# Linear attention and a routed expert layer on one core: one transfer per output tile, two x blocks per slot, a load moved to another queue, and a new written order

## The chip, the cores and the metric

The kernel runs on one core of a Trainium2 chip. The core has a matrix engine (TensorE, PE in the profile; its weight loads stand apart as PEld), a vector engine (DVE), a scalar engine (ACT), a general engine (GpSimd, POOL) and a queue engine (SyncE, SP). Each works through its own list of instructions in order and waits on semaphores for the others. Data moves between the device's memory and the on-chip memory by 16 DMA engines; transfers are issued from SP and ACT (hardware queues) and from POOL (a software queue, which can also convert the type on the way). The metric is the device time of one execution in microseconds (us).

## The reference

For 8 batches and 8 heads, with 576 positions and 64 columns a head, linear attention is computed with phi(x) = x + 1 for x > 0 and exp(x) otherwise; its result, 4608 rows of 512, is the input x of a layer of 8 experts, each of which works on every row:

```python
kv = einsum('bhsd,bhse->bhde', phi(k), v);  z = sum_s phi(k)
x  = (phi(q) @ kv) / (phi(q) . z + 1e-06)          # 4608 x 512
P  = exp(x @ w_gate - max), then 8 rounds of: rows / row sums, columns / column sums * N / E
out = sum over e of  P[:, e] * (relu(x @ w1[e]) @ w2[e])     # w1: 512x1024, w2: 1024x512
```

All inputs are float32; the kernel computes in float16 with float32 sums.

## The kernel before

**Planner.** The kernel does not issue its instructions in program order. Every piece of work is a task, added with `add` (engine, function, dependencies, priority, and the buffers it takes, `acq`, or uses, `use`); `_Plan.run` then emits the tasks engine by engine. A load is two tasks: the issue on `sp` or `pool`, and its time on a pretended engine `dma`. The order of the first part, to about 318 us, is written out in `_FRONT` (lines 139 to 213): each word is a task's number and a letter for the engine (p TensorE, a ACT, d DVE, g GpSimd, s SyncE, m dma, n none). What comes after it is chosen greedily, from the durations that each `add` states, by earliest start and then by priority. These durations and the dma tasks only shape the order. On the chip an engine waits for real semaphores: for data, and for a buffer's earlier readers.

**Attention** (`att`, 16 calls, one for each batch and group of four heads; below, the n-th k, q and v are those of call n, from 0). k, q and v come in as loads of 128 partitions. k goes into three float32 buffers `kin`, and so does q of call 0; the other q and all v are converted to float16 on the way by the software queue. Call 0's k and q and call 1's k are issued from SP (`sp = wide and b == 0`, line 370), all other loads from POOL, as are the weights. Then come exp on ACT (`ek`, `eq`), phi on DVE (`t`, `tq`), kv sums (`kv_ps`), the transposition of q (`att`, `qpT`), denominators (`rden`) and the x columns (`xT`). Before the first data PE runs 46 warm-up products.

**Experts.** Rows are taken in 9 units of 512. Expert 0 runs among the attention as far as its x is there: units 0 to 3 as plain products, later units in a form that does 7 block products in place of 8 on sums and differences of blocks, made by DVE. For experts 1 to 7 all units use the 7-product form. Its 7 blocks of x (the raw ones and the sums) are stored once per unit to a buffer in device memory (`xd`, by `x_blocks`) and loaded again for each expert by `x_load`, from SP, into a ring of ten slots `xs`. Units are grouped `SUBS = (0), (1,2), (3,4), (5,6), (7,8)`; a pair's block is one load of 256 KB, unit 0's is 128 KB and fills half of a slot. An expert thus takes 35 slots. `l1_half` takes a group's 7 loads and does the first layer (L801; `pair` holds the 7 products, read in the order 1, 5, 6, 3, 2, 7, 4); `layer2` does the second (L1095), with DVE adding P times the result into `acc` (L1126) and, for one of the seven products, ACT scaling and POOL adding (L1133, L1136). Slots 7 to 9 lie where `xT` and the routing's buffers were and open (`x_closed`) only when the routing weights `P_sb` are done, at the end of eight rounds on DVE that run beside expert 0.

**Weights.** w1 and w2 have two buffers each. A load is issued by POOL when the buffer of two experts before is free, and stands in POOL's order among the additions of L1136. Expert 0's come in halves (`parts=2`).

**End.** After the last expert's layer 2 each of a unit's four tiles of 128 rows by 512 is written out by `out_dma`: two transfers of 64 partitions, both from SP, and for unit 8 the second from ACT. Unit 8's last work (`last`) is done as five pieces, the last two of 256 columns each.

Of the kernel before, what the change touches and what calls it, by code (L numbers as in the profile page):

```python
# [17 lines left out]
class _Plan:  # L18
# [35 lines left out]
    def run(self):  # L54
# [85 lines left out]
1n 2p 3p 4p 0g 80g 5p 52g 6p 48s 49m 7p 8p 9p 10p 11p 12p 13p 14p 15p 16p 17p 76s 50s  # L140
51m 18p 19p 54a 20p 21p 22p 61n 23p 108n 78g 24p 25p 26p 27p 28p 29p 30p 31p 55d 62a 56d 63d 64d
65p 77m 82a 83d 84d 66a 53m 57n 58p 59a 60a 32p 33p 34p 35p 36p 79m 89n 90a 91d 67p 68a 81m 595n
85n 86p 92d 120g 118g 119m 37p 122g 148g 146g 109g 38p 87a 88d 121m 125d 69p 70a 71a 123m 39p 93p 94d 111g
40p 41p 74p 75d 42p 149m 124a 126d 150g 174g 176g 95p 96a 43p 44p 72p 45p 110m 73d 147m 127n 131n 133d 132a
159n 46p 97p 47p 98a 99a 113n 134d 202g 178g 128p 112m 114g 151m 206g 175m 160a 129d 161d 130d 135p 136d 177m 187n
596p 597p 100p 116g 101d 137p 138a 162d 179m 115m 207m 203m 598p 599p 139p 140a 102p 153d 103d 152a 154d 155n 141a 204g
205m 232g 106g 234g 233m 235m 163p 164a 600p 602p 604p 601d 603d 104g 605d 117m 156p 157a 606p 608p 158d 181d 144p 145d
180a 182d 236g 609a 165p 188a 166a 105m 237m 610p 607a 142p 143d 260g 261m 612p 167p 189d 190d 168a 169a 613d 183n 184p
185d 186d 191p 192d 611a 618p 172p 173d 262g 614p 615d 193p 194a 208a 170p 171d 107m 245n 263m 209d 210d 215n 217d 211n
632n 216a 616p 195p 633p 196a 634d 635p 636a 197a 246a 238a 218d 212p 213d 214d 637p 638d 219p 220d 200p 639p 292g 290g  # L150
247d 248d 201d 239d 240d 221p 222a 291m 641p 640a 642a 264g 617p 223p 293m 224a 225a 265m 198p 199d 624d 267d 241n 619p
249p 250d 273n 266a 242p 243a 244d 626a 620p 643p 320g 294g 318g 346g 274a 268d 275d 276d 348g 322g 321m 251p 252a 303n
226p 621p 644a 297d 227d 253p 622p 645p 319m 349m 296a 254a 228p 304a 646a 229d 298d 305d 269n 230p 270p 231a 271d 255a
277p 350g 376g 295m 278d 272a 374g 323m 375m 377m 331n 332a 333d 406g 647p 648a 258p 259d 666p 279p 280a 628a 256p 306d
257d 623p 281p 282a 283a 299n 665n 300p 630d 307p 301d 308d 378g 302d 324a 667a 347m 379m 359n 351m 360a 325d 361d 334d
668p 651p 309p 310a 284p 285d 326d 362d 669a 670p 653p 311p 312a 286p 287d 327n 654p 380a 335p 336d 328p 661a 313a 329d
330a 288p 289a 381d 560d 404g 407m 405m 493g 671d 353d 652p 352a 408g 460g 494m 314p 315d 337p 659a 338a 561d 672p 674p
675d 673a 339p 316p 354d 317d 355n 387n 389d 388a 491g 382d 390d 676p 678p 409m 461m 469s 462g 340a 677a 492m 463m 341a
470s 356p 363p 364d 464g 465m 471s 500s 417n 357a 679a 358a 501s 680p 410a 342p 343d 365p 366a 649p 562d 419d 344p 345d
553d 367p 368a 418a 681a 699p 383n 384p 385a 411d 386d 554d 369a 495g 496m 502s 563s 432g 433m 434g 435m 655p 391p 392a  # L160
372p 373d 412d 701p 656p 370p 371d 420d 497a 393p 394a 445n 413n 650p 414p 698n 700a 436g 415d 498d 499d 416d 702a 657a
395p 503g 396a 564m 555d 556s 558s 397a 663a 438a 437m 703p 682p 421p 400p 705p 684p 422d 439d 423p 704a 424a 401d 446a
447d 440d 574d 575d 557m 685p 398p 399d 683p 576d 577s 578m 559m 441n 476n 477a 425p 706d 426a 707p 708a 448d 692d 442p
443a 444a 709p 449p 478d 690d 450d 427a 508n 509a 479d 567d 688p 689p 451p 710a 428p 429d 581d 568d 582d 452a 569d 570s
572s 565s 571m 566m 686p 711p 453p 696a 454a 455a 466a 430p 431d 583d 713p 584s 579s 585m 588g 589n 480p 481d 510d 504n
592n 573m 687p 456p 457d 511d 712d 402p 505p 739n 403a 506a 593g 714d 507a 694d 467d 468d 512p 740p 590g 458p 459d 472n
741a 580m 513a 742p 744p 591m 514p 515a 473p 735d 474d 475d 736d 516p 517a 518a 719p 720p 482p 483a 743a 519p 520d 727d
721p 484p 485a 521p 745d 522d 737d 746p 722p 486a 747a 489p 715p 490d 738d 487p 488d 551n 731d 778d 1009s 1011s 748p 749a
729a 750p 752p 751a 779d 732d 780d 523p 524a 754p 552p 716p 733d 526d 753a 755a 786p 717p 723a 787a 525n 527p 586s 1013s
1015s 781s 800p 718p 790p 756d 734d 792p 785n 1017s 725a 791a 1010m 587m 788p 793a 801a 789a 760p 761a 836d 757d 837d 758d  # L170
528d 838d 783s 1019s 1021s 839s 796p 529d 759d 784m 804p 805a 806p 807a 766p 767a 782m 794p 802p 803a 810p 795d 797d 811d
762p 763a 840m 1022m 1014m 808p 809d 1001d 770p 771d 768p 530p 1002d 769d 531d 798p 812p 799a 813a 772p 773a 844p 845a 764p
894d 814d 846p 847a 848p 850p 858p 852p 843n 849a 859a 765a 851a 532d 815d 816d 820p 860p 818p 861a 866p 895d 853d 817d
819a 864p 854p 865a 533p 896d 897s 855d 867d 534d 824p 825a 868p 869d 862p 863a 535d 856p 857a 821a 828p 829d 870p 871a
902p 903a 826p 822p 952d 872d 827d 953d 1003d 823a 954d 955s 1012m 1018m 956m 873d 1004d 906p 830p 831a 908p 916p 876p 841s
899s 957s 909a 912p 536p 874d 537d 918p 901n 907a 875d 917a 922p 920p 594m 878p 898m 877a 919a 921a 904p 905a 923a 882p
883a 880p 881a 879a 926p 924p 538d 886p 913d 914p 927d 925d 887d 915a 910p 539p 540d 911d 884p 960p 961a 888p 889a 928p
962p 963a 959n 966p 964p 541d 885d 929a 930d 967a 965a 968p 969d 542p 543d 974p 975a 934p 970p 978p 976p 931d 971d 1020m
1016m 958m 980p 935a 977a 979a 981a 940p 972p 973a 936p 984p 544d 545p 982p 941a 932d 546d 983d 1023p 1024a 938p 985d 1025p
547d 1029p 986p 944p 937a 939a 1026a 945d 1030a 1031p 1027p 842m 900m 987a 548p 1033p 946p 947a 1028a 933d 942p 549d 1034d 1035p  # L180
1037p 1038a 988p 550d 1000n 625a 1036a 1032d 1513n 943d 1005d 1006d 1051s 1053s 1055s 1057s 1052m 1039p 989p 1043p 1054m 1514g 1056m 990p
1040a 629a 1044a 691d 1045p 1041p 996d 1047p 1065p 1048d 1042a 693d 1059s 1066a 631a 1061s 1060m 1058m 1062m 1063s 1147s 1149s 1064m 1067p
991p 1068a 1046d 1049p 992p 1071p 1072a 1073p 1069p 1074d 1075p 1050a 951a 1076d 774d 997d 1121d 1070a 993p 1077p 1079p 1081p 1078a 695d
1080a 1082a 994p 1085p 1087p 1083p 1086a 627a 1007d 1122d 728a 1084a 1089p 1088d 1123d 1090d 998d 1093p 1094a 1095p 1148m 1096a 1515m 995p
999a 1091p 1092a 1099p 1101p 1097p 1008d 1100a 1124d 1102d 1125p 1126a 1127p 1129d 1128d 1130p 1103p 1104d 1133a 1134g 1098a 1135p 1138p 1151s
1152m 1516n 1150m 1136d 1137d 1105p 1106a 1107p 1109p 1108a 1110a 1153s 1155s 1154m 1141p 1142d 1143d 1113p 1115p 1114a 1139d 1111p 1117p 1161p
1163p 1144p 834d 1116d 1118d 1119p 1157s 1131a 1112a 1156m 1162a 1167p 660a 1159s 1140d 662d 1146d 1145d 1269s 1271s 1164a 1169p 1165p 1120a
1189d 1168a 1193p 1195p 891a 1158m 1190d 1191d 1194a 664a 1198p 1201a 1166a 892a 658a 1171p 697d 1203p 1160m 1202g 1197d 1196d 1192d 1206p
1172d 1173p 1132g 1199a 1519d 1200g 1175p 1177p 1204d 1205d 1174a 1176a 1209p 1181p 1178a 1183p 1179p 1207d 1517g 1170d 1211d 1208d 1210d 1182a
# [27 lines left out]
def kernel(  # L217
# [553 lines left out]

    xst_of, xse_done, sx_users = {}, [], []

    n_load = [0]

    def x_load(d, blk, prio):
        gr = S_.grp(p_xs)
# [533 lines left out]
```

## Time and profile before

| | |
|---|---|
| median of 3 runs | 959.66 us (959.45 to 959.77) |
| the profiled execution | 959.16 us |
| its span, first to last instruction | 957.4 us |
| granted TensorE clock, mean | 0.999 |
| DMA traffic | 112.65 MB in 87908 packets |
| x loads `xs<-xd`, from SP | 196 of 256 KB, 49 of 128 KB |
| `out_dram<-acc` | 69 from SP, 5 from ACT |
| k loads `kin<-in_k_dram` | 2 from SP, 14 from POOL |

The page gives each engine's busy time and its share of the span, the span in 40 slices of about 24 us (a digit is the busy share in tenths), the DMA queues, the chain of work that ended last (followed back from the last instruction to what released it at each step), and groups of instructions with their count, mean duration and the idle time ahead of them. Times within the trace count from the span's start. A row of the timeline has its start, its length, engine, line, operation, what it writes and reads, and in brackets the idle time before it and what ended that. A matmul's modelled length includes its way through the array, so 0.44 us of issue shows as a row of 0.59.

### The profile page before, as it was taken

How to read it: one execution, taken by the hardware profiler on the slowest of the kernel's cores; microseconds unless marked ns; L12 is line 12 of the kernel's file. 1: busy time of each engine (PE TensorE's matmuls, PEld its weight loads, DVE VectorE, ACT ScalarE, POOL GpSimd, SP SyncE). 2: the span in 40 equal slices, each digit the busy share in tenths (PEclk: the TensorE clock that was granted, in tenths of full speed). 3: DMA queues.
4: the chain of work that ended last, by engine and by line, in shares of the span. 5: the costliest groups of instructions: out<-in, count | busy, mean ns of one | idle time of the engine just before them, and what ended most of it. 6: DMA issues, size and time to landing. Idle time of an engine off the chain costs nothing.

```text
span 957.4 us, 18335 instructions
## 1 busy us (share of the span) xinstructions
PE 945.6 (99%) x7008; PEld 651.5 (68%) x7008; DVE 774.1 (81%) x1499; ACT 581.8 (61%) x1034; POOL 146.3 (15%) x208
## 2 busy tenths in 40 slices
PE   8999999999999999999999999999999999999997
PEld 4565588666677666766677666766667666776665
DVE  6998999778987888778888888878887888877775
ACT  6899766676655555555555555555555555555552
POOL 6432000001111111111111111111112111111110
PEclk9999999999999999999999999999999999999999
DMA  9998663525136222652217321552217422125544
GB/s 246 262 238 208 157 163 95 154 78 122 61 75 147 77 79 61 176 121 77 63 48 163 89 78 61 139 115 71 76 49 170 116 79 61 56 78 165 165 134 132
DMA packets 87908, 112.65 MB, mean 118 GB/s; under 512 B 7436, under 2 KB 51468, under 8 KB 87820
## 3 DMA queue, kind: packets, MB, share of 16 engines
q1 hardware_dynamic: 63708, 76.77, 26.0%
q0 software_dynamic: 23712, 34.19, 19.2%
q8 instruction: 55, 0.90, 0.4%
q10 hardware_dynamic: 400, 0.52, 0.2%
q14 instruction: 33, 0.27, 0.1%
HBM read 119.69 MB, written 17.69 MB: 143 GB/s over the span
## 4 chain that ended last, share of the span: by engine, by line
PE 90%; DMA 4%; ACT 3%; DVE 2%; issue 1%; SPq 0%; POOL 0%; DVEq 0%
PE ye L1095 36%; PE hq L801 24%; PE R L801 12%; PE Zye L801 6%; PE Zye L1095 6%; PE ye L979 2%; PE hq L696 1%; DMA hb<-in_q_dram 1%; DMA w<-in_moe_w_dram 1%; DMA kin<-in_q_dram 1%; ACT eq L456 1%; DMA xs<-xd 1%; ACT rden L492 1%; PE kv_ps L422 1%; DVE xT L507 0%
## 5 line engine op out<-in xcount | busy, mean ns | idle before, releaser
L1126 DVE SCALAR_TENSOR_TENSOR acc<-ye,P_sb,acc 128x256 f32<-128x256 f32 x620 | 267.2, 479 | 126.6 <-PE ye L1095 124.5
L1095 PEld LDWEIGHTS <-S 128*128 128x128 f16 x1984 | 194.0, 98 | 46.6 <-DVE S L1066 0.2
L1095 PE MATMUL ye<-T,S 128*128 128x256 f16 x1488 | 192.8, 273 | 0.0
L1136 POOL TENSOR_TENSOR acc<-acc,st 128x256 f32<-128x256 f32 x124 | 88.9, 737 | 632.7 <-ACT st L1133 632.7
L1095 PEld LDWEIGHTS <-hb 128*128 128x128 f16 x1584 | 155.0, 98 | 42.7 <-issue 0.8
L801 PEld LDWEIGHTS <-W 128*128 128x128 f16 x1248 | 122.1, 98 | 86.8
L832 ACT ACTIVATE hb<-hq 128x512 f16<-128x512 f32 x134 | 80.0, 597 | 138.6 <-PE hq L801 133.8
L801 PE MATMUL hq<-xs,W 128*128 128x512 f16 (+1 forms) x560 | 150.0, 358 | 0.0
L801 PE MATMUL R<-xs,W 128*128 128x512 f16 (+1 forms) x560 | 150.0, 358 | 0.0
L801 PE MATMUL hq<-xs,w 128*128 128x512 f16 (+1 forms) x560 | 139.8, 358 | 1.3 <-DMA xs<-xd 1.3
L801 PEld LDWEIGHTS <-w 128*128 128x128 f16 x936 | 91.5, 98 | 60.9 <-issue 1.8
L829 ACT ACTIVATE hb<-Zye 128x512 f16<-128x512 f32 x134 | 80.1, 598 | 37.9 <-PE Zye L801 37.8
L835 DVE CUSTOM_DVE_ANT_0 hb<-hq,sx 128x512 f16<-128x512 f32 x126 | 86.6, 687 | 16.8 <-PE hq L801 16.8
L1133 ACT ACTIVATE st<-Zye,P_sb 128x256 f32<-128x256 f32 x124 | 52.5, 471 | 75.6 <-PE Zye L1095 75.6
L822 ACT COPY sx<-hq 128x512 f32<-128x512 f32 x126 | 73.6, 584 | 37.1 <-PE hq L801 37.1
L835 DVE CUSTOM_DVE_ANT_0 hb<-R,sx 128x512 f16<-128x512 f32 x126 | 86.4, 685 | 8.9 <-ACT sx L822 8.9
L818 ACT COPY Zye<-hq 128x512 f32<-128x512 f32 x134 | 77.8, 581 | 21.0 <-PE hq L801 20.8
L1066 DVE TENSOR_TENSOR S<-hb 128x1024 f16<-128x1024 f16 x124 | 84.9, 685 | 4.8 <-ACT hb L832 4.7
L801 PE MATMUL Zye<-xs,w 128*128 128x512 f16 (+1 forms) x280 | 75.0, 358 | 0.0
L826 ACT COPY sx<-R 128x512 f32<-128x512 f32 x126 | 74.4, 591 | 0.0
L1095 PE MATMUL ye<-w,hb 128*128 128x256 f16 x528 | 68.4, 273 | 0.5 <-DVE acc L1126 0.5
L1095 PE MATMUL Zye<-w,hb 128*128 128x256 f16 x528 | 68.4, 273 | 0.0
(119 smaller groups left out, 981.4 us busy)
## 6 DMA issues: line engine op xcount, KB each, us to landing
xs<-xd SPq DMA_DIRECT2D x196, 256.0 KB, 3.8
out_dram<-acc SPq DMA_DIRECT2D x67, 128.0 KB, 2.4
w<-in_moe_w_dram POOLq DMA_DIRECT2D x16, 512.0 KB, 7.9
kin<-in_k_dram POOLq DMA_DIRECT2D x14, 576.0 KB, 8.2
w<-in_moe_w_dram POOLq DMA_DIRECT2D x7, 1024.0 KB, 9.6
xs<-xd SPq DMA_DIRECT2D x49, 128.0 KB, 2.6
vv<-in_v_dram POOLq DMA_DIRECT2D x16, 288.0 KB, 7.2
hb<-in_q_dram POOLq DMA_DIRECT2D x15, 288.0 KB, 7.8
```

Source lines behind the costliest of these rows:

```text
L801: nc.tensor.matmul(dst_[:, p, :] if parts == 2 else dst_.rearrange("p a b -> p (a b)"), lhsT=lhs(p, c), rhs=blk[i](c), start=(first and p ...
L818: nc.scalar.copy(out=Zt[1], in_=gX["tile"])
L822: nc.scalar.copy(out=gs2["tile"], in_=gX["tile"])
L826: nc.scalar.copy(out=gs5["tile"], in_=gR["tile"])
L829: nc.scalar.activation(out=dst(0, 0), in_=Zt[1], func=AF.Relu)
L832: nc.scalar.activation(out=dst(1, 0), in_=gX["tile"], func=AF.Relu)
L835: nc.vector._custom_dve(TENSOR_ADD_SAT, out=out_, in0=ps, in1=sb, s0=3.0e38, s1=0.0)
L1066: nc.vector.tensor_tensor(out=Sx[:, i], in0=a0, in1=a1, op=op)
L1095: nc.tensor.matmul(bank(g_)[:, s, :], lhsT=lhs(s, kk), rhs=rhs(kk), start=(new and s == 0 and kk == 0), stop=(kk == 3), skip_group_check=True)
L1126: nc.vector.scalar_tensor_tensor(out=dst(), in0=bank(g_)[:, s, :], scalar=P_sb[:, gg, e:e + 1], in1=dst(), op0=ALU.mult, op1=ALU.add)
L1133: nc.scalar.mul(out=gst["tile"], in_=bank(g_)[:, s, :], mul=P_sb[:, gg, e:e + 1])
L1136: nc.gpsimd.tensor_tensor(out=dst(), in0=dst(), in1=gst["tile"], op=ALU.add)
```

## The change

1. **Output.** `out_dma` makes one transfer of 128 partitions per tile, or per piece of the last unit, in place of two of 64. Of `last`'s five pieces the second and fourth are issued from ACT, the others from SP.
2. **x blocks.** For unit 0 two blocks share a slot (each contiguous in its half), so its seven loads take four slots; an expert takes 32. The slots are numbered as before, round the ring of ten.
3. **Second k.** Call 1's k is issued from POOL; call 0's q and k stay on SP.
4. **Expert 2's weights** depend, in the plan, on the x loads of the first pair of expert 1.
5. **Plan.** Among dma tasks that could start, the one that became ready first is taken, not the one of lowest priority number. Some stated durations differ (x load issue 0.45 for 0.37, weight load 1.3 for 1.4, earliest start of the first software loads 4.2 for 5.2, half a dma time for a 128 KB x load).
6. **`_FRONT`** is written anew. On SP, call 0's q comes ahead of its k. POOL's order begins k1, identity, v0, q1, k2, v1, q2, q3, v2, expert 0's w1 first half, k3, w1 second half, v3, k4, q4, v4, w2 first half, k5, gate half, q5, v5, q6, k6, w2 second half; it was identity, v1, v0, q1, q2, k2, v2, q3, k3, w1 first half, w1 second half, v3, k4, q4, k5, v4, w2 first half, v5, w2 second half. Expert 2's w1 load stands on POOL behind four additions of expert 1 (units 0 and 1) in place of ahead of them; its w2 load, which stood behind those four, behind one addition more. On TensorE the first expert products keep their place after the first three calls' sums; from the 67th task to the 76th, and from about the 350th on, the two orders agree.

```diff
@@ _Plan.run
-                    if r is not None and at(e, t, r) <= te + 1e-9 and (pick is None or (t["prio"], t["id"]) < (pick["prio"], pick["id"])):
+                    if r is not None and at(e, t, r) <= te + 1e-9 and (
+                            pick is None or (t["ready"] if e == "dma" else t["prio"], t["id"]) <
+                            (pick["ready"] if e == "dma" else pick["prio"], pick["id"])):
@@ _FRONT
-1n 2p 3p 4p 0g 80g 5p 52g 6p 48s 49m 7p 8p 9p 10p 11p 12p 13p 14p 15p 16p 17p 76s 50s
...
+50s 51m 1n 61n 63d 2p 3p 4p 5p 6p 7p 8p 9p 48s 49m 10p 11p 76g 77m 62a 64d 55d 12p 13p
...
@@ att
-            sp = wide and b == 0
+            sp = n == 0 and wide
@@ x_load
-    def x_load(d, blk, prio):
-        gr = S_.grp(p_xs)
-        i = n_load[0] % NXS
-        n_load[0] += 1
-
-        def fn(_):
-            gr["tile"] = xs_t[i]
-            nc.sync.dma_start(out=xs_t[i][:, :, 0:len(SUBS[d])], in_=xd[d][:, blk])
...
+    def x_load(d, prio):
+        gx = {}
+        dbl = len(SUBS[d]) == 2
+        for m, (blk, b) in enumerate(ORD.items()):
+            h_ = 0 if dbl else m % 2
+            if h_ == 0:
+                gr = S_.grp(p_xs)
+                i = n_load[0] % NXS
+                n_load[0] += 1
+
+            def fn(_, gr=gr, h_=h_, i=i, b=b):
+                gr["tile"] = xs_t[i]
+                nc.sync.dma_start(out=xs_t[i] if dbl else xs_t[i][:, h_], in_=xd[d][:, b] if dbl else xd[d][:, b, :, 0])
...
+            def view(c, gr=gr, h_=h_):
+                return gr["tile"][:, c].rearrange("p s t -> p (s t)") if dbl else gr["tile"][:, h_, c]
+            gx[blk] = gr, td, view
+        return gx
@@ l1_half
-            st["x"] = {i: x_load(d, b, un) for i, b in ORD.items()}
+            st["x"] = x_load(d, un)
+            if n == 1:
+                first_x.extend(t for _, t, _ in st["x"].values())
@@ out_dma
-    def out_dma(g, tt, deps, c0=0, cw=DM):
-        for half in range(2):
-            def f_o(_, half=half):
-                bb, j = divmod(2 * (4 * g + tt) + half, NJ)
-                dst = AP(tensor=out.tensor, offset=(S * bb + j) * DM + c0, ap=[[NJ * DM, PW], [1, cw]])
-                eng = nc.scalar if g == NG - 1 and half == 1 else nc.sync
-                eng.dma_start(out=dst, in_=acc[g][64 * half:64 * half + 64, tt, c0:c0 + cw])
-            add(("sp", 0.45), f_o, deps=deps, prio=900.0)
+    def out_dma(g, tt, deps, c0=0, cw=DM, act=False):
+        def f_o(_):
+            o0, o1 = (S * bb + j for bb, j in (divmod(2 * (4 * g + tt) + half, NJ) for half in range(2)))
+            dst = AP(tensor=out.tensor, offset=o0 * DM + c0, ap=[[(o1 - o0) * DM, 2], [NJ * DM, PW], [1, cw]])
+            (nc.scalar if act else nc.sync).dma_start(out=dst, in_=acc[g][:, tt, c0:c0 + cw])
+        add(("sp", 0.5), f_o, deps=deps, prio=900.0)
@@ last
-            out_dma(g, tt, [t], c0, cw)
+            out_dma(g, tt, [t], c0, cw, act=i % 2 == 1)
@@ weights of later experts
-                w_t[e] = load_w1(e, prio=float(e), deps=w_t[e - 1][1][1:]) + load_w2(e, prio=float(e), deps=w_t[e - 1][3][1:])
+                w_t[e] = load_w1(e, prio=float(e), deps=w_t[e - 1][1][1:] + (first_x if e == 2 else [])) + load_w2(e, prio=float(e), deps=w_t[e - 1][3][1:])
```

More of the change, by code (lines that the diff above doesn't have):

```diff
@@ L145 @@
[L145 to L164, printed above, removed]
@@ new lines @@
+14p 15p 54a 56d 16p 17p 18p 0g 19p 20p 21p 65p 22p 595n 23p 24p 25p 26p 27p 83d 28p 82a 52g 53m
+57n 58p 59a 29p 30p 60a 66d 31p 32p 33p 84d 78g 79m 89n 90a 91d 92d 118g 119m 125d 67p 68a 34p 35p
+36p 37p 38p 39p 80g 81m 85n 124a 126d 120g 121m 113n 131n 69p 70a 40p 41p 86p 87d 71a 88d 42p 93p 132a
+43p 94d 148g 149m 122g 123m 74p 75d 108n 159n 109g 110m 95p 96a 44p 45p 146g 147m 72p 133d 73d 97p 98a 134d
+127n 128p 129d 161d 111g 112m 99a 130a 160a 135p 136d 46p 47p 150g 151m 174g 175m 100p 101d 596p 137p 138a 597p 598p
@@ new lines @@
+139p 176g 177m 178g 179m 102p 140a 599p 162d 153d 103d 114g 115m 152a 154d 155n 187n 202g 203m 163p 164d 600p 602p 604p
+605d 106g 107m 204g 205m 141a 601a 603a 156p 157d 158d 206g 207m 606p 608p 180a 181d 144p 145d 165p 182d 609a 166a 188a
+610p 611a 142p 143d 189d 190d 183n 215n 167p 612p 168a 169a 613d 184p 185d 186a 191p 192d 607a 614p 615a 172p 173d 193p
+194a 616p 170p 171d 209d 208a 210d 211n 234g 235m 232g 233m 116g 117m 262g 263m 236g 237m 632n 195p 618p 196a 633p 635p
+634d 260g 261m 217d 212p 216a 197a 218d 636a 213a 214d 637p 638d 219p 220a 200p 201d 639p 641p 642d 640a 245n 239d 221p
@@ L210 @@
[L210 to L212 removed]
+1626a 1629p 1658d 1631p 1659d 1630a 1627p 1691d 1633p 1628a 1632d 1663p 1665p 1634d 1664a 1660p 1692d 1666a 2089d 1635p 2086n 2087g 2088m 1669p
@@ L317, in load_w @@
             w_part[nm] = ti
-            ts_.append(add(("dma", len(part) * (1.4 if len(part) * len(pieces) > 2 else 2.6)), lambda _: None, deps=[ti],
+            ts_.append(add(("dma", len(part) * (1.3 if len(part) * len(pieces) > 2 else 2.6)), lambda _: None, deps=[ti],
                            use=[g, *gsw], prio=prio, lat=2.15))
@@ L387, in att @@
             tin[nm] = fadd(("dma", 1.47 if wide else 1.42), lambda _: None, deps=[ti], use=[gr, *gsw], prio=pr, lat=2.2,
-                           after=0.0 if sp else 5.2)
+                           after=0.0 if sp else 4.2)
         ge, gt = S_.grp(p_ek), S_.grp(p_t)
@@ L772 @@
     xst_of, xse_done, sx_users = {}, [], []
-    n_load = [0]
-    def x_load(d, blk, prio):
-        gr = S_.grp(p_xs)
-        i = n_load[0] % NXS
-        n_load[0] += 1
-        def fn(_):
-            gr["tile"] = xs_t[i]
-            nc.sync.dma_start(out=xs_t[i][:, :, 0:len(SUBS[d])], in_=xd[d][:, blk])
-        ti = add(("sp", 0.37), fn, acq=[gr], deps=[t for g in SUBS[d] for t in xd_done[g]] +
-                 [t_close, xs_prev[0], x_closed[0] if i >= 7 else None], prio=prio)
-        xs_prev[0] = ti
-        return gr, add(("dma", 1.0), lambda _: None, deps=[ti], use=[gr], prio=prio, lat=2.6)
+    n_load, first_x = [0], []
+    def x_load(d, prio):
[10 more added lines that the diff above has]
+                nc.sync.dma_start(out=xs_t[i] if dbl else xs_t[i][:, h_], in_=xd[d][:, b] if dbl else xd[d][:, b, :, 0])
+            ti = add(("sp", 0.45), fn, acq=[gr] if h_ == 0 else [], use=[gr] if h_ else [], deps=[t for g in SUBS[d] for t in xd_done[g]] +
+                     [t_close, xs_prev[0], x_closed[0] if i >= 7 else None], prio=prio)
+            xs_prev[0] = ti
+            td = add(("dma", 1.0 if dbl else 0.5), lambda _: None, deps=[ti], use=[gr], prio=prio, lat=2.6)
+            def view(c, gr=gr, h_=h_):
+                return gr["tile"][:, c].rearrange("p s t -> p (s t)") if dbl else gr["tile"][:, h_, c]
+            gx[blk] = gr, td, view
+        return gx
     def pair(e, un, gi, nm, parts, lhsA, lhsW, blk, dst, tA, tW, uses, xuse, th, tha, early, free):
@@ L917, in l1_half @@
             st["h"][SUBS[d][0]] = {0: r0, 1: r1}
-        blk = {i: (lambda c, i=i: gx[i][0]["tile"][:, c].rearrange("p s t -> p (s t)")[:, 0:256 * len(SUBS[d])]) for i in ORD}
+        blk = {i: gx[i][2] for i in ORD}
         for m in range(2):
```

111 lines of the change are left out of this document (60 added, 51 removed).

## The prediction

> **What bounds the kernel now.** I read the page's busy times and slices first, then busy time by stage, then the chain of work that ended last, then the rows at the three places where TensorE (PE) stands still.
>
> ```profile
> PE 945.6 (99%) x7008; PEld 651.5 (68%) x7008; DVE 774.1 (81%) x1499; ACT 581.8 (61%) x1034; POOL 146.3 (15%) x208
> ...
> DMA  9998663525136222652217321552217422125544
> ```
>
> PE is busy for 99% of the span, and the DMA engines are full in the first three slices of 24 us and nowhere else. A change of queues and order can only win time where PE waits. By stage (span of the stretch, PE, PEld, DVE, ACT, POOL, clock, DMA share, GB/s):
>
> ```profile
> 0.00:20.00 20.00, 17.75 (x112) 8.47 (x113) 11.94 (x21) 12.99 (x15) 12.78 (x24) 1.00 1.01 254
> 20.00:40.00 20.00, 18.15 (x151) 10.21 (x151) 18.43 (x30) 15.97 (x21) 9.37 (x13) 1.00 1.18 250
> 180.00:200.00 20.00, 18.68 (x107) 10.12 (x106) 12.96 (x22) 14.14 (x26) 0.00 (x0) 1.00 0.49 155
> 500.00:520.00 20.00, 20.00 (x169) 16.36 (x168) 16.09 (x32) 10.73 (x21) 4.21 (x7) 1.00 0.76 186
> 940.00:957.00 17.00, 12.15 (x88) 8.36 (x86) 9.11 (x18) 1.34 (x3) 1.41 (x2) 0.96 0.54 150
> ```
>
> At 500 us PE is gapless; so it is from 200 to 920, and there is nothing to win there. The losses are before 40, near 183 and after 952. The clock is 1.00, so no throttle enters the sum. The first place, in the chain:
>
> ```profile
> 1.75 6.84 DMA kin<-in_q_dram
> ...
> 8.62 1.17 ACT eq L456
> ...
> 11.47 10.81 DMA w<-in_moe_w_dram
> 22.28 0.14 issue
> 22.42 1.02 PE hq L696 x4
> ```
>
> Real work starts at 22.42, when the first half of expert 0's w1 has landed; until then PE runs warm-up products and a little attention. Second place, chain, GpSimd (POOL) rows and PE row:
>
> ```profile
> 178.21 0.47 DVE P_sb L581
> ...
> 179.68 5.63 DMA xs<-xd
> ```
> ```profile
> 174.51 0.62 POOL L313 DMA_DIRECT2D w<-in_moe_w_dram  x1 [60.48 <-PE hq L801]
> 176.21 0.62 POOL L313 DMA_DIRECT2D w<-in_moe_w_dram  x1 [1.08 <-issue]
> ```
> ```profile
> 185.32 0.59 PE L801 MATMUL hq<-xs,w 128*128 128x512 f16 x2 [1.32 <-DMA xs<-xd]
> ```
>
> The x blocks of unit pair (1, 2) sit in slots 7 to 9 first, which open only when the routing weights are done (DVE, end 178.68); they are issued at 178.81 into expert 2's w1 load, and PE waits 1.32 us. Third place, the output's issues and the last DVE row:
>
> ```profile
> L956 SPq DMA_DIRECT2D out_dram<-acc x69: 466/547/1703, 860.8 to 954.2; - x69
> L956 ACTq DMA_DIRECT2D out_dram<-acc x5: 473/489/555, 945.2 to 952.7; - x5
> ...
> DMA to landing us min/median/max: 2.2/2.4/5.8
> ```
> ```profile
> 952.19 0.48 DVE L1200 SCALAR_TENSOR_TENSOR acc<-hq,P_sb,acc 128x256 f32<-128x256 f32 x1 [0.39 <-PE hq L1191]
> ```
>
> The last result is ready at 952.67. ACT issues its half at 952.7, SP its half only at 954.2: SP is 1.5 us behind, with 0.55 us per issue and two issues per tile.
>
> **The change, part by part.** The profiled run took 959.16 (span 957.4 and 1.76 around it); the median of the runs is 959.66, 0.5 above it. I sum against the former and add the 0.5. A measurement of this kernel can tell 0.2%, 1.92 us.
>
> *Output.* 74 issues become 37, so 35 of SP's 69 at 0.547 go. Before 940 they lie beside PE work and are worth nothing. At the end SP is no longer behind: the last piece, which stays on SP, is issued at 952.71 instead of 954.22, 1.51 earlier. The last transfer doubles to 128 KB in one; the 64 KB one took 2.0 from issue to landing, the median over mostly 128 KB ones is 2.4. So the last landing moves from 956.23 to 954.7 to 955.1: a gain of 1.1 to 1.5; I take 1.3. The closing waits behind it (1.15 to the span's end) stay. ACT's two issues (0.49 each) have no ACT work behind them: its last row ends at 943.6.
>
> *x blocks two per slot.* Unit 0's seven 128 KB blocks use slots 0 to 3 instead of 0 to 6, so the next pair's first three blocks get slots 4 to 6, free since the front pools closed. SP has them issued long before 178, in the written order ahead of unit 6's stores. The first blocked load is then the fourth, the block that product 3 reads, in slot 7. PE needs it some 3.4 us after the product that stalls at 185.32 (its row of products starts at 188.77), while a load without a weight load beside it landed in 2.72 (issue 204.20, landing 206.92). In the new order the routing weights come later by about three PE tasks of 0.87, and between their place and that product stand 4.8 us of PE work, against 0.1 + 0.34 + 2.72 to 3.6: enough. Gain 1.32, the full stall; bounds 0 and 1.5. SP's seven issues of 0.32 to 0.45 stay seven and lie beside PE work. From 200 on there is no wait on these loads, so fewer slots per expert gain nothing more.
>
> *Expert 2's weights.* The plan's new dependency is no semaphore; what counts is POOL's order. Its w1 load goes behind the four additions of units 0 and 1, from 174.5 to about 216.7 (three additions stand at 213.96, 2.81 us), clear of the x loads. It then lands at about 222 to 225 (5.5 and 8.0 from issue before); DVE's first use is moved to about 227.5, so DVE does not stall; queued behind it are evictions (0.48 each) that PE waits for, so each us of lateness past 227.5 would cost about one. Its w2 load goes from 216.72 to behind the first addition of unit 2, about 227, and there meets x loads issued at 228.52 and 228.95. These landed at 231.22 and 231.87 and are needed at 233.95 and 234.38. Beside a weight load the row at 178.81 took 6.05 and its neighbour 6.33: landing 234.6 and 235.3, a new stall of 0.6 to 0.9 at worst, none at best. I take 0.4.
>
> *Second k on POOL, q before k on SP.* The first q is SP's first load and lands at about 4.5 instead of 8.59 (work on the first k, SP's first load now, starts at 4.59). POOL gains one issue of 0.72, placed ahead of the identity's two rows (0.5 us, wanted only at the first transposition, about 6.6). In POOL's order 10 loads instead of 11 now stand before w1's first half; DMA is saturated, and a load costs 1.42 (landings 9.15, 10.56, 11.95, 13.39 ...). That moves w1 from 22.28 to 20.86, but a bubble comes in: SP's two loads keep the engines busy to about 5.5, while the first software load's first packet came 4.18 after its issue began (2.18 to 6.36), and k's issue starts at about 1.75, so 5.93. Alone, later in the kernel, first packets come 1.3 to 1.7 after issue. Bubble 0 to 1.0; I take 0.4, nearest to the start's own row. So w1 lands at 21.2. The attention of the first heads is not late for it: its x rows end at 18.55 and 20.0 now and come 0.6 to 1.6 earlier with q first. The third v then lands at 26.6 and the sums that need it run at 27.99 now; w2's first half comes 1.4 earlier. PE's order from the 67th task on is the old one for ten tasks. Gain 1.1, bounds -0.8 and 2.2.
>
> [...]
>
> *The rest of the written order* (to about 318 us). The same PE work; 89 and 67 either-engine tasks on ACT and DVE become 90 and 66. Between 40 and 180 PE's starts lose about 7 us to small gaps where steady state would lose 2.5; I take no change, with bounds of 1.5 either way. From the 350th PE task on the two orders agree.
>
> **Sum.** -1.1 - 1.32 + 0.4 - 1.3 = -3.3. 959.16 - 3.3 = 955.86, plus 0.5: **956.4**.
>
> **Rivals.**
> 1. *POOL's descriptors come late.* For: the first software issue took 0.859 against a median of 0.716, and its 4.18 to the first packet is the longest; DVE's memsets of vv run from 1.35 to 3.10, across the new issue. Against: one row, 0.14. If nothing moves before 3.10, packets start at 7.3, a bubble of 1.8, which eats the load saved; front 0, total 957.5. [...]
> 2. *The new order also closes small gaps* at 20 to 180: a further 1.5, 954.9. For: the early gaps of 0.75 at 25.1 and 0.4 at 33.8 and 36.8 wait on ACT and DVE orders that are rewritten. Against: nothing says which way.
> 3. *The x stall only moves* to 228 and the front gives nothing: tail alone, 958.4.
> 4. *Slower: w2's second half.* It is issued three loads later on POOL (two q, one k overtake it) and lands at 38.77 + 3 x 1.42 + 0.4 = 43.4; its first user is PE's 99th task, at 46.1 less the gain, 45.0. PE is in order, so each us past 45.0 is lost; past 50.2 the kernel is slower by over 0.2%. POOL's waits ahead of it reach 4.4 each (13.2 in four, vv behind kv_ps): two exposed ones make 52.2, and 959.66 - 3.3 + 7.2 = 963.6. Against: it is issued 13.7 ahead of its landing now, so a wait must first use up that backlog.
>
> **How the numbers follow.** Forecast 0.52 (own range 955.2 to 957.7), rival 1 0.18, rival 2 0.12, rival 3 0.08, rival 4 0.10. 957.74 is the border of faster. Faster: 0.52 + 0.12 + half of rival 1 (it straddles the border) = 0.73; slower 0.10; same 0.17. Rival 2 with 0.7 of spread sets the low end, 954.2; the high end, 958.9, takes in rival 3 and leaves out rival 4.
>
> **What would show it.** Right: eq starts near 4.6 instead of 8.62; the first PE hq L696 near 21.3; no PE wait on xs near 184; SP's last output issue within 0.1 of the last DVE row and the span's end 4.7 minus 1.3 after it. Wrong: a w wait of PE between 40 and 50, a new xs wait near 233, DVE waiting for w near 226, or the first kin load of POOL landing after 8.5.

## The result and the profile after

The changed kernel takes **1069.53 us** in the median (1068.85 to 1070.01) against 959.71 us (959.45 to 959.77) for the kernel before beside it: a ratio of 1.1144, 95% interval 1.1125 to 1.1164. The forecast was 956.4 us, in a range of 954.2 to 958.9. It was wrong in sign and by 113 us.

The profiled execution took 1069.90 us. From its page, the busy times, then rows of the slices (each slice is now 26.7 us):

```profile
span 1068.1 us, 18283 instructions
...
PE 954.7 (89%) x7008; PEld 654.0 (61%) x7008; DVE 775.8 (73%) x1498; ACT 583.2 (55%) x1035; POOL 144.7 (14%) x209
...
PE   8999999989999999999999999999999987457600
...
PEclk9999999999999999999999999999999999687955
DMA  9999832362352326222722263226422321311111
GB/s 244 256 198 231 185 96 59 127 144 74 84 100 82 100 91 119 70 86 90 144 72 69 81 152 91 70 69 146 108 69 70 105 83 52 112 69 69 52 51 47
```

PE's busy time has grown by 9 us, the span by 110.7. Up to about 860 us the row of PE looks as before, but for an 8 at 214 to 240 us. Then it falls to 8, 7, 4, 5, 7, 6 and ends in two empty slices, while the DMA engines, which should be the reason, stand at one tenth and 47 to 52 GB/s. Before, the last four slices moved 132 to 165 GB/s with PE at work.

The same PE work in both traces shows where the difference arises (time at which an equal number of columns has gone through PE, changed minus before): about +0.6 at 200 us; +6.0 at 245 us and +6.3 from 270 on, then constant to 867 us; +54.6 when PE's last product starts (1006.5 against 951.9); +110.7 at the span's end, because the span now ends 61.6 us after that and ended 5.5 after it. So there are three pieces: **6.3 us by 270, nearly all of it by 245; 48.3 us in expert 7; 56.1 us of output after PE's end.**

The last two are one matter. The output's issues, by source line (minimum, median, maximum in ns), and the chain of work between 905 and 925 us:

```profile
L968 SPq DMA_DIRECT2D out_dram<-acc x35: 511/4917/9807, 867.0 to 1051.0; - x35
```
```profile
902.14 4.94 SPq L968
...
907.18 5.26 SPq L790
...
913.79 13.86 DMA xs<-xd
```

Before, 69 such issues took 547 ns in the median; now half of 35 take 4.9 us or more each. 256 KB in 4.92 us is 53 GB/s, which is the rate of the last slices. L790 is `x_load`: the x blocks of expert 7 are issued on SP between the outputs, SP reaches them late, and PE waits. PE's waits from 860 to 1010 us, by line:

```profile
PE R L813 <- DMA xs<-xd: 39.1, 3, 18.1
PE hq L813 <- DMA xs<-xd: 2.0, 2, 1.1
```

That is 41.1 of the 48.3 us. The rest is PE itself: for the same work it is busy 98.2 us (867 to 1007) in place of 91.0 (860.7 to 952.4 before), at a mean granted clock of 0.85 in place of 1.00. After PE has ended, the engines still work at 13% for 61 us (columns as in the stages shown earlier; the last three are clock, DMA share, GB/s):

```profile
1007.00:1068.00 61.00, 0.00 (x0) 0.00 (x0) 0.28 (x1) 0.00 (x0) 0.00 (x0) 0.52 0.13 50
```

Two engines of sixteen, fully busy, are a share of 0.125. The trace's packet records agree: sampled every 50 ns from 1010 to 1060 us, two packets are in flight in 89% of the samples and three in the others.

### The profile page after: what moved, and what is told of

It reads as the page before. It is cut to its first block, busy times and chain, and to the rows that moved or that the text cites. A ratio compares the mean times of both kernels' runs of the same rounds, so it can differ in the third digit from the quotient of the medians.

```text
span 1068.1 us, 18283 instructions
## 1 busy us (share of the span) xinstructions
PE 954.7 (89%) x7008; PEld 654.0 (61%) x7008; DVE 775.8 (73%) x1498; ACT 583.2 (55%) x1035; POOL 144.7 (14%) x209
## 4 chain that ended last, share of the span: by engine, by line
PE 81%; DMA 8%; DVE 2%; SPq 2%; issue 1%; ACT 0%; POOL 0%; DVEq 0%; POOLq 0%
PE ye L1107 32%; PE hq L813 21%; PE R L813 10%; PE Zye L1107 5%; PE Zye L813 5%; DMA xs<-xd 5%; PE ye L991 3%; PE hq L698 2%; DMA w<-in_moe_w_dram 1%; SPq L968 1%; DMA kin<-in_k_dram 1%; DMA vv<-in_v_dram 1%; DMA hb<-in_q_dram 1%; PE kv_ps L424 1%; SPq L790 1%
## 5 line engine op out<-in xcount | busy, mean ns | idle before, releaser
L1107 PE MATMUL ye<-w,hb 128*128 128x256 f16 x528 | 71.8, 281 | 0.5 <-DVE acc L1138 0.5
```

Of the source, the lines that this page charges most:

```text
L1107: nc.tensor.matmul(bank(g_)[:, s, :], lhsT=lhs(s, kk), rhs=rhs(kk), start=(new and s == 0 and kk == 0), stop=(kk == 3), skip_group_check=True)
```

## The experiments

**Theory.** The merged transfer's destination is written as `[[(o1 - o0) * DM, 2], [NJ * DM, PW], [1, cw]]`: its outermost dimension has two entries, the two rows of tokens that share a tile, and the profile after shows two engines' worth of work while it drains (a share of 0.13, two packets in flight in 89% of the samples). The theory, an inference of the author's from these two facts, is that the first causes the second: the two entries let two engines carry all of the output. **Rivals:** the size or the two far pieces of one transfer are slow; or the new order of SP's queue starves expert 7 whatever the output's form.

### 1. The output part undone alone, and done alone

The first keeps everything else of the change and gives `out_dma` its two transfers back. The second is the kernel before with only the merged `out_dma`.

```diff
-        def f_o(_):
-            dst = AP(..., ap=[[(o1 - o0) * DM, 2], [NJ * DM, PW], [1, cw]])
-            (nc.scalar if act else nc.sync).dma_start(out=dst, in_=acc[g][:, tt, c0:c0 + cw])
+        for half in range(2):
+            def f_o(_, half=half):
+                dst = AP(..., ap=[[NJ * DM, PW], [1, cw]])
+                eng.dma_start(out=dst, in_=acc[g][64 * half:64 * half + 64, tt, c0:c0 + cw])
```

> The changed kernel with the output part alone undone: each tile again leaves as two transfers of 64 partitions x 512, the second half of the last group on ACT; the x pairs, the second k on POOL and the new written order stay. Theory (the merged transfer's destination has only two entries in its outermost dimension, so it runs on two of the 16 DMA engines): both losses that lie behind it go, the 48.3 us in which PE waits for x blocks in expert 7 and the 56.1 us of output after PE's end. What stays is the 6.3 us that had gathered by 245: 959.7 + 6.3 = 966.0 us, 963 to 969, and the span ends 5 to 6 us after PE. Rival (the written order or the x pairs starve expert 7, whatever the output's form): above 1000 us, with PE's waits for xs near 902 and 948 still 18 us long.

> The kernel before with the merged output transfer alone (one per tile, the last group's turns on ACT); order, x blocks and loads as before. Theory (two of 16 engines): 959.7 + 48.3 + 56.1 = 1064 us, 1045 to 1080; SP's output issues take near 4.9 us in the median instead of 0.55, and PE waits for xs in expert 7. Rival (the merged transfer harms only beside the new x loads and the new order): below 1000 us.

Measured: undone alone **965.05 us** (963.6 to 966.6; ratio 1.0049, interval 1.0032 to 1.0066), done alone **1064.45 us** (one run). The two are 5.3 and 104.7 us above the kernel before beside them (959.74), and their sum, 110.0, is the loss of the whole change (109.8) to 0.2 us. The merged transfer alone is 104.7 of it; it needs neither the new order nor the x pairs. Its trace has both pieces again: 48.3 us more are lost in expert 7, and the span ends 61.3 us after PE's last product starts. The output's issues with the merge alone, and with the two transfers back:

```profile
L954 SPq DMA_DIRECT2D out_dram<-acc x35: 512/4922/9653, 861.9 to 1045.5; - x35
```
```profile
L970 SPq DMA_DIRECT2D out_dram<-acc x69: 466/547/1030, 867.6 to 961.6; - x69
```

### 2. Number of rows alone

Nothing is merged here. Each transfer of 64 rows is cut in two, once into 62 and 2, once into 56 and 8: equal numbers of transfers and bytes. Here the rows are the outermost dimension. The author's estimate, which nothing had shown so far, was that 62 rows would be as slow as the merged form, and that 56 would cost only their doubled issues.

```diff
-                eng.dma_start(out=dst, in_=acc[g][64 * half:64 * half + 64, tt, c0:c0 + cw])
+                for p0, p1 in ((0, 62), (62, 64)):      # or (0, 56), (56, 64)
+                    dst = AP(..., offset=(S * bb + j + p0 * NJ) * DM + c0, ap=[[NJ * DM, p1 - p0], [1, cw]])
+                    eng.dma_start(out=dst, in_=acc[g][64 * half + p0:64 * half + p1, tt, c0:c0 + cw])
```

> The kernel before, each 64-partition output transfer split into one of 62 rows and one of 2, nothing merged. [...] Rival (the merged form, 256 KB or two far pieces in one transfer, is what is slow; the number of rows is not): only the doubled issues cost, some 10 in the last unit at 0.55 us: 960 to 968 us.

> As the run with 62 and 2 rows, but split into 56 and 8 rows: as many transfers, as many issues, as many bytes. [...] Rival (any split, or the doubled issues, holds SP up in expert 7): as long as the run with 62 rows, whatever that is.

Measured: 62 and 2 rows **1065.05 us**, 56 and 8 rows **963.76 us** (one run each). Six rows more in a transfer cost 101 us. The size (124 against 112 KB), the two far pieces, the merging and the number of issues are all out as causes; the row count is left, and 62 rows give the time of the merged form (1064.45) to 0.6 us. Why 62 rows are slow and 56 are not was not shown. PE's waits for x blocks after 860 us come back with 62 rows (40.0 us in three waits; none with 56 rows). The run with 62 rows also shows that the long issue is not the cause but a consequence. Its issues are short (258 ns in the median); here SP waits instead for earlier outputs to land (SP's waits from 860 to 925 us), and the rate at the end is again that of two engines:

```profile
PE R L801 <- DMA xs<-xd: 40.0, 3, 20.8
```
```profile
SPq L957 <- DMA out_dram<-acc: 18.0, 16, 2.3
SPq L783 <- DMA out_dram<-acc: 5.8, 4, 2.2
```
```profile
1007.00:1060.00 53.00, 0.00 (x0) 0.00 (x0) 0.00 (x0) 0.00 (x0) 0.00 (x0) 0.50 0.13 51
```

In the changed kernel PE also loses time to its clock behind such stalls (0.50 from 908 to 924 us), to which the section on the hardware comes back.

### 3. The 5.3 us that are left: expert 2's w2 load

With two output transfers, PE's largest remaining stall lies at 235 to 242 us, beside a w2 load that POOL issues at 228.16 (227.47 in the changed kernel itself). In the changed kernel, POOL's rows and the stages around the stall:

```profile
226.80 0.73 POOL L1148 TENSOR_TENSOR acc<-acc,st 128x256 f32<-128x256 f32 x1 [9.12 <-ACT st L1145]
227.47 0.92 POOL L315 DMA_DIRECT2D w<-in_moe_w_dram  x1
```
```profile
235.00:237.00 2.00, 0.41 (x2) 0.21 (x3) 1.97 (x4) 1.08 (x2) 0.00 (x0) 1.00 1.14 284
237.00:239.00 2.00, 0.32 (x2) 0.10 (x1) 0.16 (x1) 0.00 (x0) 0.00 (x0) 0.89 1.07 338
239.00:241.00 2.00, 2.00 (x9) 1.07 (x8) 0.00 (x0) 0.00 (x0) 0.00 (x0) 0.50 0.70 267
241.00:243.00 2.00, 2.00 (x16) 1.58 (x15) 0.24 (x1) 0.57 (x1) 0.00 (x0) 0.75 0.08 29
```

The x blocks issued from 229.2 on share full engines with w2, PE waits twice (gaps of 1.95 and 1.85 us between its products), and then runs at a granted clock of 0.50 and 0.75 for four microseconds, which costs another 1.5. The experiment moves one load in the written order, on top of the first experiment:

```diff
-... 1212p 1187p 1243d 1200g 1514g 1515m 1244d ...   ... 1366d 1302a 1517g 1518m 1254g ...
+... 1212p 1187p 1243d 1200g 1514g 1515m 1517g 1518m 1244d ...   ... 1366d 1302a 1254g ...
```

> The changed kernel with two output transfers per tile, as in the first experiment (965.05 us), and in the written order expert 2's w2 load right behind its w1 load on POOL: issued near 218 instead of 228. Theory (w2 beside the x loads of pair (3, 4) makes PE wait twice, 1.6 us each, near 237, and the slow granted clock behind that adds some 1.9): w2 lands near 229, the x loads at 229 have the engines to themselves, and the 5.1 us that the first experiment lost there are back: 960.0 us, 958.5 to 961.5. Rival (those x loads are late in any case, or w2 beside w1 delays w1 and so DVE's rows on W): 963 us or more, with a PE wait left near 233 to 240.

Measured: **960.46 us** (959.27 to 961.79; ratio 1.0008, 0.9999 to 1.0017), 4.6 less than without the move. The three issues of w1 and w2 now stand together, no wait of PE is left between 205 and 250, and the clock stays at 1:

```profile
216.09 2.16 POOL L315 DMA_DIRECT2D w<-in_moe_w_dram  x3 [0.45 <-issue]
```
```profile
237.00:239.00 2.00, 2.00 (x19) 1.59 (x18) 1.87 (x5) 0.92 (x2) 0.37 (x1) 1.00 0.01 4
239.00:241.00 2.00, 2.00 (x16) 1.36 (x14) 1.81 (x4) 0.43 (x2) 0.58 (x1) 1.00 0.00 0
```

### 4. The x part and the front's part alone

Both start from the kernel before. The first takes the new `x_load` with its shared slots and nothing else. The second has only this:

```diff
-            sp = wide and b == 0
+            sp = n == 0 and wide
-1n 2p 3p 4p 0g 80g 5p 52g 6p 48s 49m 7p 8p ... 17p 76s 50s 51m 18p ...
+50s 51m 1n 2p 3p 4p 5p 6p 48s 49m 76g 77m 0g 80g 52g 7p 8p ... 17p 18p ...
```

> The kernel before with the x part alone: blocks of a single unit two per slot; written order, loads, weights and output as before. Theory (prediction's step, -1.32): the first x blocks of pair (1, 2) no longer wait for the routing weights, PE's wait of 1.32 us for xs near 184 goes, and nothing else moves: 958.4 us, 957.6 to 959.2. Rival 1 (the wait is due to expert 2's w1 load on the same engines, which stays): 959.7 us. Rival 2 (the blocks come earlier and push w1 back, DVE waits for it): 960 us or more.

> The kernel before with the front's part alone: SP loads q first, then k; the second k is the first load of GpSimd's queue; all other loads and the order of the engines' work as before. Theory of the prediction (-1.1): eq starts near 4.6 instead of 8.6, the first half of w1 lands a load earlier: 958.6 us. Theory from the changed kernel's trace: the GpSimd queue's first load lands at 7.9 and its second at 9.9, where before four loads had landed by 9.15; the DMA engines stand idle for some 0.8 us at the start, all later loads are that much later, and the two cancel: 959.4 us or slightly more, w1's first half at 22 us or later.

Measured: x pairs **958.93 us** (ratio 0.9994, 0.9985 to 1.0003), second k **960.10 us** (1.0006, 0.9997 to 1.0015). Neither can be told from no change by time, so the traces have to speak. With the x pairs the row that waited 1.32 us for x near 184 has no wait, and over that stretch PE gains 1.47 us on the kernel before:

```profile
184.83 0.59 PE L811 MATMUL hq<-xs,w 128*128 128x512 f16 x2
185.26 0.59 PE L811 MATMUL R<-xs,W 128*128 128x512 f16 x2
```

The six kernels with the old `x_load` show how far such a stall varies from one execution to the next: in five of their profiles this wait is put down to x and is 0.8 to 1.7 us long, in the sixth (second k) PE stands still for 1.0 at the same product. None of the eight with the new `x_load` has it.

Yet the median gains 0.7 only. The new `x_load` has a price at the other end, which the prediction had at nothing. Here are the last seven output issues of SP, in the kernel before and with the x pairs:

```profile
950.35 4.42 SPq L956 DMA_DIRECT2D out_dram<-acc  x7
```
```profile
949.87 5.13 SPq L966 DMA_DIRECT2D out_dram<-acc  x7
```

In both the first one starts 2.3 us before the last DVE row ends. With the x pairs one of the seven takes 1.3 us instead of 0.5, all behind it are later, and the span ends 5.40 us after the last DVE row instead of 4.70. This is no accident of one execution: the six profiles with the new `x_load` and the tail of before have 5.39 to 5.42, the two with the old one 4.70 and 4.78. Gain and price together are -0.8. In the kernel before a slow issue (0.90 us) stands just ahead of these seven, where nothing waits for it. Why one issue is slow, and why it moved, was not seen.

With the second k on GpSimd's queue the first expert product of this profile is not earlier but 0.67 later than in the profile of the kernel before (22.42):

```profile
23.09 1.02 PE L695 MATMUL hq<-xT,w 128*128 128x512 f16 x4 [1.22 <-DMA w<-in_moe_w_dram]
```

But that is within the spread: the six profiles with the old front have this product at 22.42 to 23.46, and the x pairs' profile, with the old front too, ran 1.0 us behind that of the kernel before up to 180 us. So what is shown is that the gain isn't there; a loss of 0.65 is not shown. The direction has better support. The stages from 4 to 8 us, of this kernel and then of the kernel before, show that with two loads on SP instead of three the engines move a little less at the start, though they are not idle (share 0.99 or more); over the first 12 us they move 222 GB/s, against 230 to 234 in the six profiles with the old front.

```profile
4.00:6.00 2.00, 2.00 (x11) 0.89 (x10) 0.00 (x0) 0.00 (x0) 1.95 (x3) 1.00 1.07 387
6.00:8.00 2.00, 2.00 (x11) 0.89 (x10) 1.53 (x3) 1.97 (x2) 0.51 (x1) 1.00 0.99 281
```
```profile
4.00:6.00 2.00, 2.00 (x7) 0.62 (x5) 0.97 (x2) 1.16 (x1) 1.50 (x2) 1.00 1.03 406
6.00:8.00 2.00, 2.00 (x9) 0.89 (x8) 0.55 (x1) 0.00 (x0) 1.95 (x3) 1.00 1.13 299
```

### 5. What the written order costs between 60 and 100 us

In the profile of the first experiment, the load of q12 (the thirteenth attention call's q) stands behind those of v12 and k14 on POOL; it is issued at 73.3, lands at 81.2, and PE waits 2.1 us near 80 behind DVE rows that need it. In the next run its word in the order goes ahead of that call's v; in the run after it, k13 and k15 change places as well:

```diff
-... 408g 409m 460g 461m 406g 407m ...
+... 406g 407m 408g 409m 460g 461m ...
-... 679a 491g 492m 493g 494m ...  445n 412d 432g 433m ...
+... 679a 432g 433m 493g 494m ...  445n 412d 491g 492m 500s 501s 502s ...
```

> As the run with w2 early, and in the written order one load more is moved: q of the thirteenth attention group (q12) goes ahead of that group's v on POOL, so that it is issued near 66 instead of 73.3. Theory (in the changed order this load lands at 81.2, and DVE and then PE wait 2.1 us for it near 80): 1.5 to 2 us less than the run with w2 early, 958.0 to 958.5 us if that gives 960.0. Rival (the next load in line, the thirteenth or fourteenth k or v, is as late): the same as the run with w2 early within 0.5 us, the stall sits at 85 to 100.

> As the run with w2 and q12 early (959.13 us), and k of the fourteenth and of the sixteenth attention group (k13, k15) change places in the written order: k13 is issued near 77 instead of 86. Theory (PE's last wait of the changed order before 100, 1.7 us behind an eviction of DVE that stands behind the late k13, goes): 957.5 us, 957.0 to 958.2. Rival (v13, issued near 93 in both, is needed as soon, or k15 comes too late instead): 959.1 us within 0.5.

> As the run with w2, q12 and k13 moved, and the second k goes back from GpSimd's queue to SP's, behind q and the first k: the second-k part of the change is undone alone. Theory (on GpSimd's queue it costs 0.65 us at the start, as the kernel before with that part alone showed in w1's landing): 0.4 to 0.8 us less than the run without this, w1's first half lands near 21.5. Rival (q first is what costs, not k's queue): the same within 0.3 us.

Measured: q12 early **959.13 us** (0.9995, 0.9986 to 1.0004), 1.3 less than without it, short of the theory's 1.5 to 2, and the two intervals overlap. The wait that it was to remove, 2.1 us in the first experiment, was also only 0.4 in the profile of the run with w2 early, so how much of the 1.3 is this load is not shown. Its trace still has the next late load, PE's wait of 1.7 behind k13. With k13 early **960.04 us** (957.97 to 963.6; 1.0013, 1.0001 to 1.0026): no gain, later than theory and rival had it, and a spread of 5.6 us. With the second k back on SP besides **959.76 us** (1.0006, 0.9997 to 1.0016): 0.3 less than the run before it, which between such spreads decides nothing (w1's first half lands at 21.31, in that run at 21.57). The profiled execution of the k13 run is its shortest (957.97) and has no such wait; the profile of the run with k on SP shows what can take its place:

```profile
96.31 0.42 DVE L743 TENSOR_TENSOR acc<-xT 128x512 f16<-128x512 f16 x1 [2.93 <-DMA xd<-acc]
```

k15 now lands at 90.19 (88.91 in the k13 run). SP, in order, waits for it with a small gate transfer (issued 90.20) before it issues `xd<-acc` at 91.14; DVE waits for that store, and PE for DVE (2.9). One late load was exchanged for another. Behind the wait the granted clock reads 0.50 and 0.74 for four microseconds (100 to 104 us), and PE loses 4.2 us on the kernel before between 90 and 101. The mean clock hints that this wait also makes the long executions of the k13 run: it is 0.996 or 0.997 in the five of them above 961.5 us and in the profile with the wait, 0.998 or 0.999 in the seven others. No long execution of that kernel was profiled, so this is not shown.

### 6. The lag at the end, and all of it together

The prediction's -1.3 for the output rested on SP being 1.5 us behind at the end. That can be had without merging:

```diff
-                eng = nc.scalar if g == NG - 1 and half == 1 else nc.sync
+                eng = nc.scalar if g >= NG - 2 and half == 1 else nc.sync
```

> The kernel before with one edit: the second half of every output tile of the last two groups goes out on ACT instead of that of the last group alone. Nothing is merged. This prices the gain that the prediction gave the merged transfer (-1.3 us: SP no longer 1.5 us behind at the end) by another way to the same effect. Theory (SP's lag of 1.5 us at the end is real and on the path): the last issues leave within 0.7 us of DVE's last row at 952.7, 958.4 us, 958.0 to 958.8. Rival (the last transfers wait for the DMA engines or ACT is late by as much): 959.7 us.

> All that has been found together: two output transfers per tile, the last two groups' second halves on ACT; x pairs; w2, q12 and k13 moved; the second k on SP. If the terms add (959.13 - 1.5 - 0.6 - 1.3): 955.7 us, 955.0 to 956.7, faster than the kernel before by 0.3 to 0.5%. Rival (each gain is taken by the next wait): 957.5 us or more.

Measured: **959.00 us** (0.9998, 0.9989 to 1.0006) and **959.77 us** (1.0004, 0.9995 to 1.0013). The lag itself goes: the issues near the end now leave from both queues side by side, the last SP issue starts at 952.86 instead of 954.22, the last on ACT at 953.18.

```profile
950.99 2.44 SPq L956 DMA_DIRECT2D out_dram<-acc  x4
950.99 2.74 ACTq L956 DMA_DIRECT2D out_dram<-acc  x4
```

But the span ends 4.28 us after the last DVE row instead of 4.70: issues that end 1.04 us earlier bring 0.42, since the end comes 3.26 us after the last issue's end instead of 2.61. The time of 959.00 lies between theory and rival. In the run with everything together the terms don't add, as its rival had it. The stall behind the k15 gate (2.5 us in its profile, 3.7 lost with the slow clock behind it) eats what the other parts bring; and the end brings nothing, for although its last issue leaves as early, the span ends 5.43 us after the last DVE row. Why the last transfers land later beside the new `x_load` was not seen. No version here beats the kernel before by more than a measurement can tell.

## Why the prediction was wrong, step by step

- **Output: -1.3 forecast, +104.7 measured.** This is the step that failed. It priced the merged transfer as "the last transfer doubles to 128 KB in one; the 64 KB one took 2.0 from issue to landing", and so assumed that a transfer's time depends on its bytes. The durations used were those of 64-row transfers (0.547 us to issue, 2.0 and 2.4 to landing). The new destination has two entries outermost, and no row of the profile of before had such a shape. The step counted issues (34 of SP's 69 go, not 35, which changes nothing) and looked only at the last one; "before 940 they lie beside PE work and are worth nothing" holds for issues of 0.55 us and not for 4.9. No rival covered it either: a slower output was not among them. The right question, how many engines a transfer of the new shape keeps busy (two packets in flight and 53 GB/s in the profile after), was asked nowhere. Even without this, the gain was too large: removing the lag on SP by another way brought 0.42 us in the trace, as the transfers then landed later behind their issues.
- **x blocks two per slot: -1.32 forecast, right for the stall, incomplete for the kernel.** No PE wait is left near 184 in any of the eight profiles, and 1.47 us are gained there in the trace of that part alone. The step had no price behind 200 us; an output issue that is slower with the new `x_load` takes 0.7 back at the end. By time alone the part can't be told (0.9994).
- **Expert 2's weights: +0.4 forecast, about +4.6 measured.** The place was right: the sign named, "a new xs wait near 233", came at 234.8. The size was not, nor was its bound of 0.9. The step took one load's landing beside a weight load and one wait; in fact several x loads in a row were late, PE waited 1.95 and 1.85, and the clock dropped behind it for another 1.5. That w1 would not hold DVE up was right.
- **Second k on POOL, q first: -1.1 forecast, no gain in that part alone (+0.4 in its median, within the noise).** In the changed kernel eq does start at 4.61 as said (alone, with ACT's old order, only at 7.10). But w1's first half lands at 22.21 there, and at 22.96 in the part alone, instead of 21.2. The first expert product of the five profiles with the whole new front is at 22.09 to 22.48, against 22.42 to 23.46 in the six with the old one: a gain of about 0.5, not 1.1. The bubble, priced at 0.4, did not show: the software queue's first packet came 3.55 us after its issue and not 4.18, and the engines' share stays at 1.01 or more from 4 to 8 us. What failed is the row of landings 1.42 apart: the first software load landed at 7.91, the second at 9.94, 2.03 later. That is 0.6 us; the rest of what is missing stays open. Rival 1, with a front of 0, came nearest in price, but its mechanism, nothing moving before DVE's memsets end and first packets at 7.3, is shown by no run: in the changed kernel the memsets run from 1.35 to 3.10 and the software queue's first packet comes at 5.21. In the changed kernel k3 also stands between w1's halves, and PE waits 1.08 for the second one near 27.
- **Rest of the written order: 0, bounds 1.5.** At equal PE work the first experiment's profile loses 3.1 us between 61 and 101 us of the kernel before, that with w2 early 1.8, that with q12 early 1.0; PE's waits there stand behind late loads. Moving one of them went with 1.3 less in the median. In the first of these profiles the bound was too narrow. Rival 2, that the order closes gaps, had the sign wrong for this stretch.
- **Rival 4, w2's second half of expert 0,** played no part: PE has no wait of that kind between 40 and 50.

By the medians: +104.7 for the output, +4.6 for w2, and +0.7 that remain of the first experiment's 5.3 for the x pairs, the front and the order together, are 110.0; the whole change measured 109.8.

## What to carry to other kernels

Before two transfers are made into one, write out the new access pattern and look at its outermost dimension: here it was 2, and the 128 rows under it moved at the rate of two engines (53 GB/s). Then ask what else issues from the same queue: here slow stores made late loads, for which PE waited 41.1 us. A weight load moved clear of one burst of loads has to be followed to the burst that it meets next, and a stall of PE like that one (busy 0.73 of 4 us) is to be priced with the slow clock that followed it (0.50 and 0.75 for 4 us, another 1.5 us). And a part that is right where it was aimed, as the x pairs were, still has to be followed to the end of the kernel.

## What the runs showed of the hardware beyond what was expected

- **Engines and row count.** Output in 62 rows took 1065.05 us for the kernel, in 56 rows 963.76. With 62 rows the end moves 51 GB/s at a share of 0.13, which is 2.1 of 16 engines, and in the changed kernel 50 GB/s at the same share; with 64 rows it is 163 GB/s at 0.60 (950 to 962 us of the first experiment). How many engines carry a transfer of 56 or of 64 rows can't be read from these shares, and what in the row count decides it was not shown.
- **A queue that is issuing can be what is blocked.** The same shortage shows as 4.92 us in the median inside the issue instruction in one kernel (merged), and as SP's waits for earlier outputs in the other (62 rows; 18.0 and 5.8 us from 860 to 925), with the same time of the kernel to 0.6 us.
- **A second price of a stall.** Around the two w2 waits PE was busy 0.73 of 4 us, and the granted clock then read 0.50 and 0.75 for the next 4 us. In expert 7 it read 0.50 from 908 to 924 around one wait of 18 us. Behind the k15 gate PE was busy 1.08 of 4 us, with 0.50 and 0.74 after it. The single wait of 1.3 us near 184 in the kernel before left it at 1.00. What length of stall brings the slow clock on, and what ends it, was not shown. Of the 48.3 us lost in expert 7, the waits explain 41.1, and the 7.2 by which PE's busy time grew there, at a mean clock of 0.85, explain the rest.
